# Softplus and SiLU as single ScalarE activations, and new durations and lags for the kernel's list scheduler

## The chip, the cores and the metric

The kernel runs on one core of one Trainium2 chip. The metric is the device time of one execution in microseconds, the median of several. The core has TensorE (PE, matrix multiplication into PSUM), VectorE (DVE), ScalarE (ACT), GpSimd (POOL) and SyncE (SP), whose queue issues all the DMAs of this kernel.

## The reference

```python
# q, k, v: [2, 8, 768, 64]; proj: [64, 6]
mask = bucket(q @ proj) == bucket(k @ proj)       # 6 sign bits for each row
scores = where(mask, q @ k.T / sqrt(64), -1e9)
attn = exp(scores - max) / (sum + 1e-9)
x = (attn @ v) as [1536, 512]                      # heads side by side
h = x @ w_in                                       # [512, 2048]
g = maximum(h, 0) + log1p(exp(-abs(h)))            # softplus
x = g @ w_out                                      # [2048, 512]
gate = x @ w_gate;  val = x @ w_val                # [512, 1536] each
out = (gate * 1 / (1 + exp(-gate)) * val) @ w_out2 # [1536, 512]
```

The weights come as 64-bit floats, read as pairs of 32-bit words.

## The kernel before

The 1536 rows are cut into four chunks of 384 (two batches, two halves each). Three stages follow each other, with overlap:

- Attention: for each batch, head and 128-row tile ("unit", 96 in all) PE makes the scores into PSUM tile `z`, DVE takes their minimum or maximum (`mx`, L888/L893), ACT takes the exponential with its row sum (`ex`, L909), the result is turned (on PE, or split in two f16 halves by ACT/POOL and turned by a DMA, `PT<-P`), and PE applies the values (`pv`). Chunk 0 works in fp32, the others with f16 halves.
- First feed-forward (`ffn1`, once for each chunk): 16 tiles of 128 hidden rows x 384 columns, twelve f16 matmuls each (L1134 to L1136, in the helper `three`), into a PSUM bank of ring `f` or, in batch 1, of `f` and `z` by turns (two banks each). The softplus of a tile is: Abs on ACT (`mag`, L1161), relu on DVE or ACT (`relu`, L1166), Exp and Ln on ACT (`ex`, L1177; `ln`, L1180), their sum on DVE (`add`, L1183), then a high half (`hi`, L1188 on ACT, L1194 on POOL) and a low half (`lo`, L1197 on POOL) in f16. Then four accumulations of 48 matmuls each with `w_out`.
- Gated unit: the products with `w_gate` and `w_val` are Strassen products of 2 x 2 blocks, for which batch p's input is first scaled, subtracted and split (`parts7`, L1274 to L1323), and each weight piece too (`split7`). `pair_of` runs for each batch and each of six column groups: seven products per matrix, their sums by ACT (`keep`, L1463) and DVE (`plus`, L1468), then for four tiles a Sigmoid (L1497/L1499), a multiplication with the gate itself, one with the value (`mul`, L1502; `mul_raw`, L1505, for the tile that is still in PSUM), the halves (L1510, L1513), and the last products with `w_out2` (L1537 to L1539) that DVE adds up (L1553).

The weights of the first feed-forward come in 16 pieces: two DMAs into the one buffer `raw64a`, three integer operations on DVE (L408, L413, L419) that make 32-bit floats, a sum of squares on ACT and a one-column matmul on PE for the scale (`total`, L359), and the two halves (L446 to L462).

The order of all instructions is made by a list scheduler when the program is built (`Order`). A step has an urgency, one or several ways to run (engine, cost in us, function, and perhaps a bonus or malus from the table `BV`), the steps it comes after, and the buffers it takes from rings of fixed size. `run` keeps a model of when each engine is free, takes the steps that could start first, and among those that start within SLACK of the first the one with the lowest urgency; each engine gets its instructions in that order and then runs them in order on the chip. `LAT` is the lag from an engine's end to another's start ("EA": PE to ACT; W and V are both DVE), `dve`, `stt`, `act`, `gps`, `gts` and `pe` are costs of an operation of n columns, `U` shifts the urgency of kinds of steps, and `T0`, `GAP`, `LEAD`, `W1_GAP`, `W2_GAP` set when units and weight pieces come due.

Of the kernel before, what the change touches and what calls it, by code (L numbers as in the profile page):

```python
# [55 lines left out]
class Order:  # L56
# [132 lines left out]
def tile_hash_attention__softplus_ffn__silu_glu(  # L189
# [54 lines left out]
    BV = dict(ck=0.865, re=1.809, st=-2.309, tf=0.612, th=1.227, hi=2.138, lo=5.114, slo=0.082, wlo=0.046, bits=-0.999, meas=1.623, cv=-0.593, ca=0.592)  # L244
    U = dict(st=0, vl=0, tp=-20.24, th=-2, tl=-1.85, w2=51.64, qp=-7.63, kp=-4.93, kv=3.56, f1=0.25, y=40, ev=-5.28, ex=2.63, hi=-7.89, lo=2.67, gw=422.36, x=3.11)
# [1498 lines left out]
```

## Time and profile before

| | us |
|---|---|
| median of 3 runs (lowest, highest) | 880.66 (879.75, 881.27) |
| the profiled execution | 882.55 |
| its span, first to last instruction | 880.6 |
| mean granted clock of TensorE | 0.972 of full speed |

The rows below are of that one execution. PE's busy time counts matmuls in flight; they overlap, so the duration of one is longer than the time from one to the next. A granted clock below 1.00 in a stretch is the share of full speed that was granted over that stretch; the levels are 1.0 (2.4 GHz) and 0.5 (1.2 GHz).

### The profile page before, as it was taken

What the parts mean: (1) busy time and instruction counts of PE and PEld (TensorE: products, weight loads), DVE (VectorE), ACT (ScalarE), POOL (GpSimd) and SP (SyncE); (2) the same over time, 40 slices, a digit from 0 to 9 for tenths busy, and PEclk for the clock granted to TensorE, in tenths of its full rate; (3) what the DMA queues carried; (4) which work ended last, traced back from release to release, by engine and by line L of the source; (5) the groups of instructions that cost most, each with busy time, mean ns of one, the idle gap of its engine ahead of it and who ended that gap; (6) DMA issues with size and microseconds to landing.
All of it is one profiled execution on the core that took longest, in us unless ns stands there. A gap on an engine that the chain in (4) does not pass through costs nothing.

```text
span 880.6 us, 14652 instructions
## 1 busy us (share of the span) xinstructions
PE 811.8 (92%) x5436; PEld 517.1 (59%) x5436; DVE 653.8 (74%) x1188; ACT 501.9 (57%) x966; POOL 473.1 (54%) x453
## 2 busy tenths in 40 slices
PE   7999899889989988998889998995899999999998
PEld 4666567456555655565556565563566566666666
DVE  4788687979896769879547798329858989694445
ACT  3455365568887677885667658335455545353331
POOL 0001111769786678885668737416745675764332
PEclk9999799989999999999989999998999999999999
DMA  6244344856778887666773421000312121200003
GB/s 203 75 132 136 114 115 118 170 124 128 169 131 169 163 163 136 103 88 128 129 130 58 156 96 49 1 1 8 136 48 95 49 96 48 96 1 1 1 1 143
DMA packets 179191, 86.05 MB, mean 98 GB/s; under 512 B 141104, under 2 KB 165808, under 8 KB 179120
## 3 DMA queue, kind: packets, MB, share of 16 engines
q1 hardware_dynamic: 179120, 85.12, 41.2%
q8 instruction: 42, 0.69, 0.3%
q14 instruction: 29, 0.24, 0.1%
HBM read 47.35 MB, written 3.15 MB: 57 GB/s over the span
## 4 chain that ended last, share of the span: by engine, by line
PE 46%; DVE 27%; DMA 12%; POOL 5%; issue 5%; ACT 3%; SPq 1%; DVEq 0%; POOLq 0%; ACTq 0%
DMA PT<-P 7%; PE z L1134 5%; PE z L1136 5%; PE z L1135 5%; PE z L869 4%; PE f L1537 3%; PE f L1539 3%; PE f L1538 3%; PE f L602 3%; DVE fr L1183 2%; PE pv L966 2%; DMA raw64a<-in_moe_w_in_dram 2%; POOL P L929 2%; DVE E L888 2%; DVE fr L1166 2%
## 5 line engine op out<-in xcount | busy, mean ns | idle before, releaser
L929 POOL TENSOR_TENSOR P<-E,P 128x768 f16<-128x768 f32 x72 | 123.6, 1718 | 14.0 <-ACT P L916 10.5
L1502 POOL TENSOR_TENSOR sg<-cc,sg 128x384 f32<-128x384 f32 x45 | 51.0, 1144 | 69.8 <-DVE cc L1468 32.9
L869 PE MATMUL z<-k,q 128*128 128x384 f32 x192 | 81.4, 554 | 3.5 <-DVE E L888 3.5
L1134 PE MATMUL z<-y,w 128*128 128x384 f16 x216 | 71.4, 331 | 12.3 <-DVE cc L1468 4.2
L1197 POOL TENSOR_TENSOR g<-fr,g 128x384 f16<-128x384 f32 x64 | 67.1, 1055 | 17.3 <-ACT g L1188 13.2
L1463 ACT ACTIVATE cc<-z,smalls 128x384 f32<-128x384 f32 x72 | 40.4, 576 | 55.2 <-PE z L1136 54.9
L1513 POOL TENSOR_TENSOR sT<-sg,sT 128x384 fp32r<-128x384 f32 x48 | 59.8, 1263 | 21.4 <-ACT sT L1510 21.4
L1136 PE MATMUL z<-y,w 128*128 128x384 f16 x216 | 71.2, 330 | 0.0
L1135 PE MATMUL z<-y,w 128*128 128x384 f16 x216 | 71.2, 330 | 0.0
L1134 PE MATMUL f<-xy,w1h 128*128 128x384 f16 x192 | 63.9, 333 | 2.5 <-DVE smalls L371 1.4
L1537 PE MATMUL f<-wo,sT 128*128 128x512 f32 x144 | 62.2, 432 | 3.3 <-DVE acc L1553 2.6
L909 ACT ACTIVATE E<-E,st 128x768 f32<-128x768 f32 x48 | 44.7, 931 | 35.3 <-DVE E L888 33.3
L1135 PE MATMUL f<-xy,w1h 128*128 128x384 f16 x192 | 64.0, 333 | 0.0
L1136 PE MATMUL f<-xy,w1l 128*128 128x384 f16 x192 | 63.9, 333 | 0.0
L966 PEld LDWEIGHTS <-PT 128*128 128x128 f16 x1296 | 47.4, 100 | 25.2 <-DMA PT<-P 15.2
L1183 DVE SCALAR_TENSOR_TENSOR fr<-fa,smalls,fr 128x384 f32<-128x384 f32 x64 | 56.0, 886 | 6.3 <-ACT fa L1180 4.0
L966 PE MATMUL pv<-v,PT 128*128 128x64 f16 x1296 | 51.4, 196 | 10.0 <-DMA PT<-P 9.6
L1539 PE MATMUL f<-wo,sT 128*128 128x512 f32 x144 | 56.4, 392 | 0.0
L1538 PE MATMUL f<-wo,sT 128*128 128x512 f32 x144 | 56.3, 391 | 0.0
L888 DVE TENSOR_SCALAR_CACHE_REDUCE E<-z 128x768 f32<-128x768 f32 x48 | 45.5, 953 | 14.5 <-PE z L869 9.0
L1135 PEld LDWEIGHTS <-w 128*128 128x128 f16 x336 | 33.2, 99 | 36.7 <-issue 18.8
L1553 DVE TENSOR_TENSOR acc<-f,acc 128x512 f32<-128x512 f32 x60 | 41.2, 687 | 16.6 <-PE f L1539 14.9
(253 smaller groups left out, 2288.7 us busy)
## 6 DMA issues: line engine op xcount, KB each, us to landing
raw64a<-in_moe_w_in_dram SPq DMA_DIRECT2D x16, 512.0 KB, 4.4
raw64a<-in_moe_w_out_dram SPq DMA_DIRECT2D x16, 512.0 KB, 5.0
raw64b<-in_moe_w_gate_dram SPq DMA_DIRECT2D x12, 512.0 KB, 4.4
raw64b<-in_moe_w_val_dram SPq DMA_DIRECT2D x12, 512.0 KB, 4.7
raw64b<-in_moe_w_out_dram SPq DMA_DIRECT2D x12, 512.0 KB, 4.4
rawk<-in_k_dram SPq DMA_DIRECT2D x19, 192.0 KB, 2.8
rawv<-in_v_dram SPq DMA_DIRECT2D x19, 192.0 KB, 2.9
rawq<-in_q_dram SPq DMA_DIRECT2D x16, 192.0 KB, 3.9
```

The source lines that it names most:

```text
L869: nc.tensor.matmul(a[:, x, 0:HS], lhsT=plain(qd["q"])[:, ts], rhs=plain(kd["k"])[:, x * HS:(x + 1) * HS], start=True, stop=True,)
L888: nc.vector.tensor_scalar(new(att, [128, 2, HS], F32, E), z.t[:, :, 0:HS], PLAIN_TOP, None, op0=ALU.min, op1=ALU.min, accum_out=a[:, 1:2],)
L929: return lambda: eng.tensor_tensor(P.t[:, 1, :], E.t.rearrange("p a b -> p (a b)"), P.t[:, 0, :], op=ALU.subtract)
L966: nc.tensor.matmul(pv.t[:, t, :], lhsT=PT.t[:, w, kk, :], rhs=values.t[:, kk, c0:c0 + D], start=(kk == 0 and w == 0 and c0 == 0), stop=(kk ...
L1134: nc.tensor.matmul(ps, lhsT=wh, rhs=xh, start=first, stop=False, skip_group_check=onto)
L1135: nc.tensor.matmul(ps, lhsT=wh, rhs=xl, start=False, stop=False, skip_group_check=onto)
L1136: nc.tensor.matmul(ps, lhsT=wl, rhs=xh, start=False, stop=last, skip_group_check=onto)
L1183: nc.vector.scalar_tensor_tensor(out=fr.t, in0=fa.t, scalar=sc[b]["sg"], in1=fr.t, op0=ALU.mult, op1=ALU.add)
L1197: return lambda: eng.tensor_tensor(g.t[:, 1], fr.t, g.t[:, 0], op=ALU.subtract)
L1537: nc.tensor.matmul(f.t, lhsT=sT.t[:, 0, cs], rhs=wh, start=(r == 0), stop=False)
L1538: nc.tensor.matmul(f.t, lhsT=sT.t[:, 0, cs], rhs=wl, start=False, stop=False)
L1539: nc.tensor.matmul(f.t, lhsT=sT.t[:, 1, cs], rhs=wh, start=False, stop=(r == 1))
```

## The change

In batch 1 the softplus is one Softplus activation into `fa`; the high half is taken from it with the scale `sg` (ACT, POOL or DVE), the low half by one scaled subtraction on DVE or two operations on POOL. Each Softplus comes after all Exp and Ln steps that were made before it (`all_exps`): those of attention, and of batch 0's softplus, which stays as it was. In the gated unit Sigmoid and the multiplication with the gate become one Silu. The scheduler's lags, its cost functions, many single costs, `BV`, `U` and the due times have new numbers. The core of the diff (single costs of other steps change in the same manner):

```diff
-    LAT = {"EE": 0.0, "AA": 0.15, "GG": 0.1, "VV": 0.13, "EA": 0.2, "EV": 0.2}
+    LAT = {
+        "EE": 0.0, "AA": 0.15, "GG": 0.1, "VV": 0.13, "EA": 0.22, "EV": 0.2, "EG": 0.25, "AV": 0.125, "VA": 0.115,
+        "GV": 0.035, "GA": 0.035, "AG": 0.17, "VG": 0.23, "AE": 0.145, "VE": 0.135, "GE": 0.06,
+    }
...
     def act(n):
-        return 0.28 + n / 1400.0
+        return 0.09 + n / 1200.0
     def gps(n):
-        return 0.1 + n / 510.0
+        return 0.143 + n / 526.0
     def gts(n):
-        return 0.05 + n / 1050.0
+        return 0.28 + n / 1211.0
...
-    BV = dict(ck=0.865, re=1.809, st=-2.309, tf=0.612, th=1.227, hi=2.138, lo=5.114, slo=0.082, wlo=0.046, bits=-0.999, meas=1.623, cv=-0.593, ca=0.592)
-    U = dict(st=0, vl=0, tp=-20.24, th=-2, tl=-1.85, w2=51.64, qp=-7.63, kp=-4.93, kv=3.56, f1=0.25, y=40, ev=-5.28, ex=2.63, hi=-7.89, lo=2.67, gw=422.36, x=3.11)
+    BV = dict(ck=0.788, re=0.248, st=-4.032, tf=1.16, th=-3.479, hi=3.915, lo=12.565, slo=-0.738, wlo=-0.612, bits=-4.056, meas=4.769, cv=-0.383, ca=0.101)
+    U = dict(st=-1.482, vl=-21.844, tp=-33.571, th=-50.907, tl=14.878, w2=44.101, qp=4.699, kp=-5.538, kv=0.27, f1=16.662, y=42.77, ev=-43.888, ex=6.594, hi=-11.632, lo=13.78, gw=250.452, x=2.144)
...
-            s = x = step(u + U["ex"], "A", act(S) + 0.39, ex, [s], uses=[E, st, sums], line="ex")
+            s = x = step(u + U["ex"], "A", act(S) + (0.2 if PLAIN[b] else 0.29), ex, [s], uses=[E, st, sums], line="ex")
+            all_exps.append(x)
...
-                s = step(u + U["tp"], "E", 6 * 0.14, turn, [s], takes=[T], uses=[E], line="tp")
+                s = step(u + U["tp"], "E", 0.68, turn, [s], takes=[T], uses=[E], line="tp")
...
+            def soft(gi=gi, f=f, fa=fa):
+                nc.scalar.activation(
+                    new(gpool, [128, CN], F32, fa), f.t[:, 0:CN], AF.Softplus, scale=sc[b]["inv"][:, gi:gi + 1]
+                )
+            def thi_a(fa=fa, g=g):
+                nc.scalar.activation(g.t[:, 0], fa.t, AF.Copy, scale=sc[b]["sg"])
...
+            def tlo_v(fa=fa, g=g):
+                nc.vector.scalar_tensor_tensor(
+                    out=g.t[:, 1], in0=fa.t, scalar=sc[b]["sg"], in1=g.t[:, 0], op0=ALU.mult, op1=ALU.subtract
+                )
+            def tlo_g(fa=fa, g=g):
+                nc.gpsimd.tensor_scalar(fa.t, fa.t, sc[b]["sg"], 1.0, op0=ALU.mult, op1=ALU.mult)
+                nc.gpsimd.tensor_tensor(g.t[:, 1], fa.t, g.t[:, 0], op=ALU.subtract)
...
+            if b == B - 1:
+                a = step(U["f1"], "A", act(CN) + 0.07, soft, [s, g_ready] + exps, takes=[fa], uses=[f])
+                a = ways(U["f1"], [("A", act(CN) + 0.09, thi_a), ("G", gts(CN), thi_g), ("W", dve(CN, 2), thi_v)], [a], uses=[fa, g])
+                g_done.append(ways(U["f1"], [("G", gts(CN) + gps(CN), tlo_g), ("W", stt(CN), tlo_v)], [a], uses=[fa, g]))
+                continue
...
-            a = step(U["f1"], "A", act(CN) + 0.04, ln, [a], uses=[fa])
+            a = step(U["f1"], "A", act(CN) + 0.1, ln, [a], uses=[fa])
+            all_exps.append(a)
...
-            return ways(u, [("W", dve(n) + 0.05, go(nc.vector)), ("G", gps(n) + 0.15, go(nc.gpsimd), BV["lo"])], after)
+            return ways(u, [("W", dve(n) + 0.05, go(nc.vector)), ("G", gps(n), go(nc.gpsimd))], after)
...
-                    nc.scalar.activation(t, tg.t, AF.Sigmoid)
+                    nc.scalar.activation(t, tg.t, AF.Silu)
...
-            for n, t, e in (("g", tg, None), ("v", tv, ends[1][j])):
-                if raw:
-                    s = step(0, "V", stt(CN) + 0.08, mul_raw(n, t), [s, e], uses=[t, sg])
-                else:
-                    s = ways(0, [("W", dve(CN), mul(nc.vector, t), 0.3), ("G", gps(CN) + 0.1, mul(nc.gpsimd, t))], [s, e], uses=[t, sg])
+            if raw:
+                s = step(0, "V", stt(CN), mul_raw, [s, ends[1][j]], uses=[tv, sg])
+            else:
+                s = ways(0, [("W", dve(CN), mul(nc.vector)), ("G", gps(CN), mul(nc.gpsimd))], [s, ends[1][j]], uses=[tv, sg])
...
-    T0, GAP, LEAD, W1_GAP, W2_GAP = 12, 2.65, 12.351, 5.974, 6.601
+    T0, GAP, LEAD, W1_GAP, W2_GAP = 15.591, 2.644, 12.522, 4.542, 2.827
```

## Rows read from the trace of the kernel before

**Rows 1.** The page's busy shares: us, share of the span, instructions.
```profile
PE 811.8 (92%) x5436; PEld 517.1 (59%) x5436; DVE 653.8 (74%) x1188; ACT 501.9 (57%) x966; POOL 473.1 (54%) x453
```

**Rows 2.** Stages: length, busy us of PE, PEld, DVE, ACT, POOL, clock, DMA share, GB/s.
```profile
22.00:154.00 132.00, 123.60 (x671) 86.94 (x672) 104.39 (x216) 68.22 (x122) 16.23 (x21) 0.95 0.37 115
154.00:449.00 295.00, 267.72 (x2399) 163.00 (x2397) 232.47 (x465) 210.93 (x434) 216.22 (x205) 0.97 0.75 140
449.00:586.00 137.00, 131.07 (x867) 79.09 (x866) 87.78 (x124) 83.95 (x167) 78.01 (x80) 0.98 0.26 67
...
594.00:616.00 22.00, 12.90 (x63) 6.52 (x61) 21.79 (x29) 12.38 (x21) 14.40 (x9) 0.84 0.03 4
...
638.00:858.00 220.00, 213.91 (x1167) 140.58 (x1167) 161.05 (x250) 99.75 (x177) 121.67 (x111) 0.99 0.13 44
```

**Rows 3.** The same view: two stretches of 22 us in the first feed-forward.
```profile
528.00:550.00 22.00, 19.27 (x109) 11.08 (x107) 18.41 (x28) 18.46 (x37) 17.31 (x19) 0.92 0.14 49
572.00:594.00 22.00, 22.00 (x138) 13.38 (x137) 4.37 (x11) 8.07 (x16) 3.03 (x2) 1.00 0.00 1
```

**Rows 4.** Groups of PE, 449 to 586: count, busy us, mean ns, idle before.
```profile
L966 PE MATMUL pv<-v,PT 128*128 128x64 f16 x92 | 3.7, 194 | 0.9 <-DMA PT<-P 0.9
```

**Rows 5.** Groups of ACT, 449 to 562, by form.
```profile
L1180 ACT ACTIVATE fa<-fa,smalls 128x384 f32<-128x384 f32 x32 | 19.4, 612 | 0.5
L1177 ACT ACTIVATE fa<-fa 128x384 f32<-128x384 f32 x32 | 16.4, 518 | 0.5
L1161 ACT ACTIVATE fa<-z,smalls 128x384 f32<-128x384 f32 x16 | 9.2, 577 | 5.3 <-DVE fr L1183 4.7
```

**Rows 6.** Groups of DVE, 449 to 562, by form.
```profile
L1183 DVE SCALAR_TENSOR_TENSOR fr<-fa,smalls,fr 128x384 f32<-128x384 f32 x32 | 24.7, 777 | 3.0 <-ACT fa L1180 0.9
L1166 DVE TENSOR_SCALAR fr<-z,smalls 128x384 f32<-128x384 f32 x16 | 9.8, 613 | 8.3 <-POOL g L1197 6.7 <-ACT fa L1161 1.5
```

**Rows 7.** Groups of POOL over the span.
```profile
L1197 POOL TENSOR_TENSOR g<-fr,g 128x384 f16<-128x384 f32 x64 | 67.1, 1055 | 17.3 <-ACT g L1188 13.2 <-PE pv L966 1.0 <-DVE xp L582 0.6
...
L1502 POOL TENSOR_TENSOR sg<-cc,sg 128x384 f32<-128x384 f32 x45 | 51.0, 1144 | 69.8 <-DVE cc L1468 32.9 <-DVE sg L1502 19.9 <-ACT sg L1499 16.8
...
L1194 POOL TENSOR_SCALAR g<-fr 128x384 f16<-128x384 f32 x34 | 19.8, 586 | 15.2 <-DVE fr L1183 15.1
```

**Rows 8.** Groups of DVE over the span: the two multiplications.
```profile
L1502 DVE TENSOR_TENSOR sg<-cc,sg 128x384 f32<-128x384 f32 x27 | 17.6, 662 | 3.0 <-ACT sg L1499 3.0
...
L1505 DVE SCALAR_TENSOR_TENSOR sg<-z,smalls,sg 128x384 f32<-128x384 f32 x24 | 14.6, 610 | 0.5 <-PE z L1136 0.5
```

**Rows 9.** ACT in order of time: start us, us, then the instruction.
```profile
451.57 0.58 ACT L1161 ACTIVATE fa<-f,smalls 128x384 f32<-128x384 f32 x1 [0.18 <-PE f L1136]
...
453.66 0.19 ACT L909 ACTIVATION_READ_ACCUMULATOR E<-E,st,smalls 128x1 f32 x1
```

**Rows 10.** PE in order of time, with its idle time.
```profile
543.30 0.38 PE L359 MATMUL f<-smalls 128*128 128x1 f32 x2 [1.28 <-DVE fr L1166]
545.13 0.32 PE L1134 MATMUL f<-xy,w1h 128*128 128x384 f16 x1 [1.44 <-DVE smalls L371]
```

**Rows 11.** Groups of PE, 594 to 616.
```profile
L1134 PE MATMUL z<-y,w 128*128 128x384 f16 x19 | 6.9, 365 | 9.1 <-DVE sg L1505 4.1 <-ACT cc L1463 3.4 <-DVE cc L1468 1.6
```

**Rows 12.** ACT in order of time, around the table load.
```profile
597.99 1.28 ACT L1499 ACT_TABLE_LOAD   x1
599.28 0.52 ACT L1499 ACTIVATE sg<-cc 128x384 f32<-128x384 f32 x1
```

**Rows 13.** One line, L408: ns min/median/max, first and last start.
```profile
L408 DVE TENSOR_SCALAR w32a<-raw64a x16: 679/694/1584, 10.2 to 223.1; 128x1024 int32<-128x1024 int32 x16
```

**Rows 14.** Groups of DVE, 22 to 154: the other operations of a weight piece.
```profile
L419 DVE SCALAR_TENSOR_TENSOR w32a<-raw64a,w32a 128x1024 int32<-128x1024 int32 x11 | 13.8, 1251 | 0.2
L413 DVE SCALAR_TENSOR_TENSOR w32a<-raw64a,w32a 128x1024 int32<-128x1024 int32 x11 | 13.5, 1223 | 0.1
L462 DVE SCALAR_TENSOR_TENSOR w1l<-w32a,smalls,w1h 128x1024 f16<-128x1024 f32 x8 | 10.2, 1278 | 0.7 <-POOL w1h L458 0.7
```

More of the change, by code (lines that the diff above doesn't have):

```diff
@@ L359, in go @@
             nc.tensor.matmul(f.t[:, 0:n], lhsT=ones_mat, rhs=t, start=True, stop=True)
-        return order.step(urgency, [("E", 0.45, go)], after, [f]), f
+        return order.step(urgency, [("E", 0.22, go)], after, [f]), f
     def pow2(r):
@@ L642, in planes @@
         for x, f in enumerate(ps):
-            s = step(u, "E", pe(4 * HS if plain else 2 * HS), products(x, f), after, takes=[f], uses=uses)
-            b = ways(u, [("V", dve(HS) + 0.14, bits(x, f), BV["bits"]), ("A", act(HS), signs(x, f))], [s],
+            s = step(u, "E", 0.85 if plain else 0.4, products(x, f), after, takes=[f], uses=uses)
+            b = ways(u, [("V", dve(HS) + 0.14, bits(x, f), BV["bits"]), ("A", act(HS) + 0.09, signs(x, f))], [s],
                      takes=[hb[x]], uses=[f] + uses)
@@ L781, in copy @@
             return go
-        s = step(u, "E", 6 * 0.14, turn, [ld[0]], takes=[T, kk], uses=[raw[0]], line="tk")
-        s = ways(u, [("A", act(S) - 0.05, copy(nc.scalar.copy)), ("V", dve(S) + 0.07, copy(nc.vector.tensor_copy), BV["ck"])],
+        s = step(u, "E", 0.68, turn, [ld[0]], takes=[T, kk], uses=[raw[0]], line="tk")
+        s = ways(u, [("A", act(S) - 0.04, copy(nc.scalar.copy)), ("V", dve(S) + 0.07, copy(nc.vector.tensor_copy), BV["ck"])],
                  [s], uses=[T, kk])
@@ L807, in copy_v @@
             nc.vector.tensor_scalar_mul(plain(qq)[0:64], T.t[0:64, 0:CN], -1.0 / float(D) ** 0.5)
-        s = step(u, "E", 3 * 0.14, turn, [ld], takes=[T, qq], uses=[raw], line="tq")
-        s = ways(u, [("A", act(CN), copy_a), ("V", dve(CN) + 0.13, copy_v, BV["ck"])], [s], uses=[T, qq])
+        s = step(u, "E", 0.36, turn, [ld], takes=[T, qq], uses=[raw], line="tq")
+        s = ways(u, [("A", act(CN) + 0.02, copy_a), ("V", dve(CN) + 0.05, copy_v, BV["ck"])], [s], uses=[T, qq])
         pl = planes(u + U["qp"], 1, 1, lambda: plain(qq)[0:64], lambda: plain(qq), [s, proj_ready], [], [qq], True)
@@ L849, in tile_hash_attention__softplus_ffn__silu_glu @@
     xn_open = {}
+    all_exps = []
     turned = []
@@ L985, in apply_f @@
                     )
-            s = step(u, "E", pe((8 if PLAIN[b] else 4) * HS), qk, kd["ready"] + qd["ready"], takes=[z], uses=[kd["k"], qd["q"]],
+            s = step(u, "E", 1.32 if PLAIN[b] else 0.68, qk, kd["ready"] + qd["ready"], takes=[z], uses=[kd["k"], qd["q"]],
                      line="qk", behind=turned[-2:-1])
-            s = step(u, "V", dve(S) + 0.15, mx, [s, first, hs.get("iv")],
+            s = step(u, "V", dve(S) + 0.1, mx, [s, first, hs.get("iv")],
                      takes=[st, E] + ([sums] if t == 0 else []), uses=[z] + ([sums] if t else []), line="mx")
@@ L1492, in pair_of, with silu, mul, mul_raw @@
             raw = j == 2
[L1494 removed]
+            def silu(tg=tg, sg=sg, raw=raw):
                 t = new(late["f2"], [128, CN], F32, sg)
                 if raw:
[L1497 removed]
+                    nc.scalar.activation(t, tg.t[:, 0, 0:CN], AF.Silu, scale=gvs[b, "g"][:, mp:mp + 1])
                 else:
[L1499 to L1506 removed]
+                    nc.scalar.activation(t, tg.t, AF.Silu)
+            def mul(eng, sg=sg, tv=tv):
+                return lambda: eng.tensor_tensor(sg.t, tv.t, sg.t, op=ALU.mult)
+            def mul_raw(sg=sg, tv=tv):
+                nc.vector.scalar_tensor_tensor(
+                    out=sg.t, in0=tv.t[:, 0, 0:CN], scalar=gvs[b, "v"][:, mp:mp + 1], in1=sg.t, op0=ALU.mult, op1=ALU.mult
                 )
@@ L1692, in finish @@
             s = step(due, "A", act(n), hi_a, [s, f2_open], takes=[slot], uses=[w32], line="wo")
-            return None, ways(due, [("G", gps(n) + 0.1, lo(nc.gpsimd)), ("W", dve(n), lo(nc.vector), BV["lo"])], [s], uses=[w32, slot])
+            return None, ways(due, [("G", gps(n), lo(nc.gpsimd)), ("W", dve(n), lo(nc.vector), BV["lo"])], [s], uses=[w32, slot])
         return finish
```

87 lines of the change are left out of this document (42 added, 45 removed).

## The prediction

> **What bounds the kernel now.** I read the page's busy shares first: TensorE (PE) has a matmul in flight for 92% of the span, VectorE (DVE) works 74%, ScalarE (ACT) 57%, GpSimd (POOL) 54% [rows 1]. An average over stages says little, so next I cut the span into stages [rows 2]. The reader is to see three things there. From 22 to 449 us (attention of both batches, with the first feed-forward of batch 0 fitted in) PE is without a matmul for 132.00 - 123.60 + 295.00 - 267.72 = 35.7 us, and the granted clock is 0.95 and 0.97: the missing 5% and 3% are 6.6 + 8.9 = 15.5 us of clock, which is the time lost if all of it was spent at the lower level (1.2 GHz) with PE full. From 449 to 586 (first feed-forward of batch 1) DVE, ACT and POOL are all under 65% busy, so PE is the bound. In 594 to 616 PE has 12.90 us and DVE 21.79 of 22: there DVE is the bound. From 638 to 858 PE is idle 6.1 us of 220: the gated unit there runs at PE's pace.
>
> Busy PE is not PE at its peak, so I take the peak from a stretch that is full: 138 matmuls, nearly all of 384 columns, in 22 us at clock 1.00 are 0.159 us each [rows 3]. In 449 to 586 there are 867 matmuls, 92 of them short attention ones [rows 2, 4]; the other 775, all but a few of 384 columns, need 123 us. The 92 short ones, at their share of a pipelined run, add about 3 us (estimate; their 194 ns of [rows 4] overlap). So 137 - 126 = 11 us of that stage is lost. In 594 to 616 the 63 matmuls need 10.0 us, so 12.0 is lost.
>
> **Part A, Softplus for batch 1.** Removed for each of 32 tiles: on ACT Abs (577 ns), Exp (518) and Ln (612); on DVE the relu (613) and the sum (777) [rows 5, 6]. Added: one Softplus on ACT. The trace has no Softplus; every 384-wide activation in the group takes 518 to 612 ns whatever its function, and the one with the same operands (PSUM in, a scale from a tile) takes 577, which I use. So ACT sheds 32 x (0.518 + 0.612) = 36.2 us. DVE sheds 32 x (0.613 + 0.777) = 44.5 us, and takes back at most 32 x 0.78 = 25 us if all low halves go to it. The low half goes to POOL today at 1055 ns [rows 7]; there it now needs the scaling too, 586 + 1055 = 1.64 us, so the planner will give most to DVE, and POOL sheds up to 34 us. None of that is time by itself: a tile needs 12 x 0.159 = 1.91 us of PE, and ACT spends 1.71 us on it now. What it buys is the waits of PE that these operations end: ahead of 543.30 PE stands 1.28 us for a DVE relu and ahead of 545.13 it stands 1.44 us for small DVE operations behind the next relu [rows 10], and that window's clock is 0.92, or 1.8 us of 22 [rows 3]. I take the two gaps and the clock, and half a microsecond for smaller waits on the relu: -5. Bounds: 0 (if weight pieces keep DVE busy at the same places) and -11 (everything lost).
>
> **Part A's new wait.** A Softplus waits for every Exp and Ln planned so far, that of the last attention unit too. Queued behind it on ACT in program order is whatever the planner put there; who waits is PE, for the PSUM banks that unread tiles hold: two "f" and two "z". In the run the first Abs of chunk 2 starts at 451.57 and the last Exp's accumulator read ends at 453.85 [rows 9]. With a table load behind that (1.28 us [rows 12]) the first Softplus starts at 455.1, 3.6 us later than today's Abs. Four banks are four tiles, 7.6 us of PE, so in today's order the banks cover it and the cost is 0. They no longer do so if chunk 2's tiles are ready more than 7.6 us ahead of the last Exp, and a held "z" bank is one that the last attention units, which also use two, don't have. I take +1; bounds 0 and +8 (three more units of the run of Exps, at the planner's 2.64 us of spacing).
>
> Of the load, the row says that the old gated stage's one load took 1.28 us, from 597.99 to 599.27, and the Sigmoid ran right behind it [rows 12]. The Trainium skill ("ScalarE: Activation LUTs", What ACT_TABLE_LOAD costs) puts a switch at about 2.66 us, since it counts a drain of 1.38 us beside the load. By the row the added switch costs ACT 1.3 us, by the page 2.7; with the four-bank cover the sum is the same to within 1.4 us, and the trace shows no such drain.
>
> **Part B, Silu.** Sigmoid and Silu are one activation each, with one table load; what goes is the first of two multiplications for each of 48 tiles. 12 are the DVE form at 610 ns (half of the 24): 7.3 us. 36 are half of the 72 L1502, 45 on POOL at 1144 ns and 27 on DVE at 662: (51.0 + 17.6) / 72 = 0.95 us each, 34.3 us [rows 7, 8]. In 594 to 616 PE's 9.1 us of waits end on exactly these: 4.1 on the raw multiplication, 3.4 on the ACT copy, 1.6 on the DVE add [rows 11]. The raw tile's bank is freed by the Silu instead of the multiplication behind the sigmoid, about one DVE operation sooner (0.6 to 0.9 us), and DVE has some 3 us less to do. But most of DVE's 21.79 us is the preparation of batch 1's Strassen operands, which stays. I take -3; bounds -12 (all lost there) and +4 (the new plan puts three or four POOL operations of 1.14 us ahead of what PE waits for). In 638 to 858 only 6.1 us can be had; I take -2, bounds -6 and 0, since POOL and DVE are off PE's path there.
>
> **Part C, the planner's numbers.** Outside A and B no operation is added or removed; what changes is order and which engine takes an operation with several ways. The old costs were off: a 384-wide activation was planned at 0.28 + 384/1400 = 0.55 us and takes 0.52 and, back to back, less; the POOL scaling was planned at 0.42 + 0.06 and takes 0.586 [rows 5, 7]. With ACT cheaper and its bonus "re" cut from 1.81 to 0.25, more relus of batch 0 go to ACT: each takes 0.61 us off DVE. Where it can pay is 22 to 449, where 35.7 us of gaps and 15.5 us of clock lie. The errors were tens of nanoseconds against steps of 0.5 to 2 us, and DVE is 79% busy there in each part [rows 2], so I expect few of the gaps to go: -6. Bounds: -51 (all) and +19, the slow rival below.
> The same part moves transfers: the pieces of w_in and w_out come due every 4.5 and 2.8 us instead of 6.0 and 6.6, and w_out starts at 44 instead of 52. Each piece has two DMAs on SP's queue, and they are moved past the loads of k, q and v; the one raw64a buffer holds each next pair until DVE has read the last, which limits how far they can run ahead. I cost the DMAs at nothing, covered by the DMA share of 0.37 in 22 to 154 [rows 2]; without the cover a late q, k or v would stop a unit.
>
> **Sum.** -5 + 1 - 3 - 2 - 6 = -15. The profiled execution took 882.55 us (span 880.6 and 1.95 around it): 867.5. The median of the runs is 880.66, 1.89 less: **866**. Adding the ends of all terms gives far more than the chance of them meeting, so the range is made from the cases below.
>
> **Rivals.**
> 1. The plan gains a lot. If half of the 51 us of gaps and clock in 22 to 449 goes, C is -25, the sum -34: 847. For it: no engine is full there, so the losses are order. Against: DVE's 79% is in bursts, and PE can't wait less than its DVE reader.
> 2. The gate eats the gain. The last Exp comes late against chunk 2, four banks are full, and the tail of attention runs with one "z" bank: +8 instead of +1, and nothing from C: -5 + 8 - 3 - 2 = -2: 879. For it: an f1 tile of batch 1 is already there ahead of the last Exp; against: 3.6 us stand against 7.6 us of cover.
> 3. Slower: weight pieces crowd early attention. A piece costs DVE 0.69 + 1.22 + 1.25 + 1.28 = 4.4 us [rows 13, 14]. 16 pieces run from 10.2 to 223.1 us; 11 lie in 22 to 154, one ahead, so four lie behind 154. Brought ahead of 154 they are 4 x 4.4 = 18 us more for a DVE that is busy 104 of 132 us, in the one stretch where PE has no feed-forward to fill with; nothing comes back if the later stretch is held by POOL (216 of 295 us) as much as by DVE. +18 and -9 from the others: 890. It decides when more than about half of that work lands where DVE has no idle time; for it: the new gaps of 2.8 us; against: the single raw64a buffer.
> 4. It doesn't do what it says: Softplus needs its own table, and the Squares between its tiles switch it back and forth. Row: the old gated stage has Sigmoid, Square and Copy in turn and one load [rows 12]. The trace has no Softplus to tell the same of its set; six alternations of two loads would be 12 x 1.28 = 15 us of ACT, inside the 36 it sheds, with some stalls of PE: 870. The Trainium skill ("ScalarE: Activation LUTs", Table sets: the hidden batching unit) says that cheap functions stand in every set; by that rule there is one more load and nothing else, and the Sigmoid row agrees.
>
> **How the numbers follow.** Forecast (856 to 874, with rival 4 in it): 0.44. Rival 1 (under 856): 0.20. Rival 2 (874 to 882): 0.15, of which 0.07 is within 0.2%, that is within 1.8 us of 880.66, about what a measurement of this kernel can tell from no change. Rival 3 (over 882): 0.21. So faster 0.44 + 0.20 + 0.08 = 0.72, same 0.07, slower 0.21. The range goes from 846, just under rival 1, to 887, short of rival 3's price: about 0.08 is left out below and 0.11 above. The forecast's own range is 856 to 874.
>
> **What would show it.** A: in the profile after, between the first Softplus and the gated unit, PE without the two gaps and with a clock near 1.00; 32 fewer Exps and Lns. Gate: PE's idle time just ahead of the first Softplus, and who ends it. B: PE's idle in the 20 us behind the last feed-forward matmul, now 9.1 us. C: the time of the last Exp, now 453.85; if it is over 460 rival 3 is right, under 435 rival 1. I am wrong altogether if the stages behind the last Exp get longer, or if more than three table loads show.

## The result and the profile after

The changed kernel takes 847.58 us (median of four runs, 843.72 to 850.67); the kernel before, on the same chip, 880.2. The ratio is 0.9631 [0.9586, 0.9676], or 32.6 us less. The direction is as forecast and the time lies inside the range (846 to 887), but below the forecast's own 856 to 874, and the change is more than twice the 15 us of the sum: as a forecast of size it was wrong.

I cut every profile into four stages at the same events: 22 us; chunk 0's first feed-forward matmul; chunk 2's first one (in these two profiles the last Exp of attention is beside it; in others it comes up to 18 us earlier); the end of the last `w_out` matmul of chunk 3; the end. For the profiled executions (882.55 and 850.67 us):

| us | early attention | late attention | feed-forward of batch 1 | gated unit | span |
|---|---|---|---|---|---|
| before | 147.1 | 280.0 | 137.3 | 294.2 | 880.6 |
| after | 134.1 | 277.5 | 129.2 | 286.2 | 849.0 |
| difference | -13.0 | -2.5 | -8.1 | -8.0 | -31.6 |

The page's busy shares of after, to set against [rows 1]: POOL sheds 128 us and DVE 41.5, ACT almost nothing.

```profile
PE 794.6 (94%) x5436; PEld 511.7 (60%) x5436; DVE 612.3 (72%) x1151; ACT 499.9 (59%) x950; POOL 344.8 (41%) x320
```

The view by stretches (length, then busy us of PE, PEld, DVE, ACT, POOL, the granted clock, DMA share, GB/s), first of the kernel before, for its two attention stages as cut here:

```profile
22.00:169.10 147.10, 136.33 (x737) 93.49 (x737) 118.44 (x234) 76.21 (x136) 28.07 (x30) 0.94 0.41 118
169.10:449.10 280.00, 255.09 (x2333) 156.52 (x2333) 218.51 (x447) 202.94 (x420) 204.47 (x196) 0.97 0.75 140
```

Then of after; the last three lines answer to the last three of [rows 2]:

```profile
22.00:156.10 134.10, 129.09 (x759) 91.27 (x760) 116.26 (x237) 86.02 (x153) 19.12 (x23) 0.97 0.49 133
156.10:433.60 277.50, 250.35 (x2328) 155.29 (x2328) 214.81 (x434) 224.01 (x458) 176.42 (x160) 0.98 0.75 142
433.00:563.00 130.00, 128.73 (x868) 78.72 (x869) 70.44 (x116) 53.24 (x100) 22.36 (x21) 1.00 0.24 67
571.00:593.00 22.00, 16.99 (x88) 9.47 (x88) 21.37 (x38) 13.03 (x24) 8.17 (x7) 0.92 0.14 48
...
615.00:827.00 212.00, 209.39 (x1150) 138.24 (x1149) 145.66 (x234) 96.58 (x172) 95.90 (x85) 1.00 0.13 43
```

In early attention PE's idle time went from 10.8 to 5.0 us and the clock's share (the part of full speed that was not granted, times the length) from 8.8 to 4.0: 10.6 of the 13.0 us. In batch 1's feed-forward PE is idle 1.3 us of 130 at full clock, where it was idle 5.9 of 137 at 0.98. The gated unit starts at 0.92, where it was 0.84, and then has a full clock.

**Softplus.** Groups of PE of after from 433 to 563 us (busy us, mean ns, then idle before and what ended it): the matmuls of the tiles and of `w_out` wait for nothing (the one wait that the stage has, 1.1 us, is ahead of a scale matmul of a weight piece).

```profile
L1139 PE MATMUL z<-g,w2h 128*128 128x384 f16 x128 | 41.7, 326 | 0.0
...
L1139 PE MATMUL f<-xy,w1h 128*128 128x384 f16 x64 | 20.9, 326 | 0.1
```

Groups of ACT of after, 433 to 545, by form. A Softplus takes 578 ns, as taken from the Abs of [rows 5]; seven high halves are ACT's, the other 25 DVE's.

```profile
L1182 ACT ACTIVATE fa<-f,smalls 128x384 f32<-128x384 f32 x16 | 9.3, 579 | 13.7 <-PE f L1141 13.0 <-DVE g L1196 0.7
L1182 ACT ACTIVATE fa<-z,smalls 128x384 f32<-128x384 f32 x16 | 9.2, 578 | 15.1 <-PE z L1141 15.1
L1335 ACT ACTIVATE junk<-xy 128x384 bf16<-128x384 f32 x12 | 6.2, 518 | 0.2
L1187 ACT ACTIVATE g<-fa,smalls 128x384 f16<-128x384 f32 x7 | 4.3, 615 | 0.2
```

Groups of DVE of the same stretch: all 32 low halves went to DVE, none to POOL.

```profile
L1196 DVE SCALAR_TENSOR_TENSOR g<-fa,smalls,g 128x384 f16<-128x384 f32 x32 | 21.4, 670 | 5.2 <-ACT g L1187 4.4
L1190 DVE TENSOR_SCALAR g<-fa,smalls 128x384 f16<-128x384 f32 x25 | 10.4, 418 | 17.2 <-ACT fa L1182 17.2
```

ACT of after in order of time (start, duration, instruction): the gate that the forecast priced. The last Exp's accumulator is read at 433.32, the table loaded at 435.74, and the first Softplus runs at 437.04. PE's groups above show that nobody waited.

```profile
433.32 0.19 ACT L913 ACTIVATION_READ_ACCUMULATOR E<-E,st,smalls 128x1 f32 x1
...
434.89 0.83 ACT L920 CAST P<-E 128x768 f16<-128x768 f32 x1 [1.39 <-DMA PT<-P]
435.74 1.28 ACT L1182 ACT_TABLE_LOAD   x1
437.04 0.58 ACT L1182 ACTIVATE fa<-f,smalls 128x384 f32<-128x384 f32 x1
437.65 0.61 ACT L1187 ACTIVATE g<-fa,smalls 128x384 f16<-128x384 f32 x1
```

The whole trace has three table loads, at 0.79, 435.74 and 579.68 us; the twelve Squares (L1335) between Softplus tiles cause none, so rival 4 is out. The Trainium skill ("ScalarE: Activation LUTs", Table sets: the hidden batching unit) has cheap functions in every set; the trace agrees for Copy (the seven of L1187) and for Square, which that section of the Trainium skill doesn't list.

**Silu.** Of 96 multiplications 48 are left; POOL's of after over the span, to set against [rows 7]:

```profile
L1536 POOL TENSOR_TENSOR sg<-cc,sg 128x384 f32<-128x384 f32 x14 | 17.0, 1226 | 42.0 <-ACT sg L1533 31.2 <-PE f L1572 8.0 <-DVE cc L1502 2.8
```

and DVE's, against [rows 8]:

```profile
L1536 DVE TENSOR_TENSOR sg<-cc,sg 128x384 f32<-128x384 f32 x22 | 15.2, 690 | 0.7
...
L1539 DVE SCALAR_TENSOR_TENSOR sg<-z,smalls,sg 128x384 f32<-128x384 f32 x12 | 7.3, 608 | 0.0
```

Where PE stood 9.1 us at the start of the gated unit, 4.1 of them for the raw multiplication [rows 11], it now stands 6.2, and no multiplication is among what ended it there (PE of after, 571 to 593):

```profile
L1139 PE MATMUL z<-y,w 128*128 128x384 f16 x24 | 8.3, 348 | 6.2 <-ACT cc L1497 4.9 <-ACT sg L1531 0.9 <-DVE cc L1502 0.5
```

### The profile page after: what moved, and what is told of

Its sections match the earlier page's. It is cut to its first block, busy times and chain, and to the rows that moved or that the text cites. A ratio compares the mean times of both kernels' runs of the same rounds, so it can differ in the third digit from the quotient of the medians.

```text
span 849.0 us, 14355 instructions
## 1 busy us (share of the span) xinstructions
PE 794.6 (94%) x5436; PEld 511.7 (60%) x5436; DVE 612.3 (72%) x1151; ACT 499.9 (59%) x950; POOL 344.8 (41%) x320
## 4 chain that ended last, share of the span: by engine, by line
PE 35%; DVE 11%; ACT 5%; DMA 3%; POOL 3%; issue 2%; SPq 0%; POOLq 0%; DVEq 0%; ACTq 0%
PE z L1139 6%; PE z L1141 6%; PE z L1140 6%; PE f L1570 3%; PE f L1572 3%; PE f L1571 3%; DMA PT<-P 2%; DVE w L1420 2%; DVE cc L1502 1%; PE f L1139 1%; PE f L1140 1%; PE f L1141 1%; PE y L1139 1%; PE y L1141 1%; PE y L1140 1%
## 5 line engine op out<-in xcount | busy, mean ns | idle before, releaser
L873 PE MATMUL z<-k,q 128*128 128x384 f32 x192 | 76.8, 528 | 3.1 <-DVE E L892 3.0
L1139 PE MATMUL z<-y,w 128*128 128x384 f16 x216 | 71.2, 329 | 8.5 <-ACT cc L1497 6.4
L1139 PE MATMUL f<-xy,w1h 128*128 128x384 f16 x192 | 63.9, 333 | 7.0 <-DVE fr L1171 4.1
L897 DVE TENSOR_SCALAR_CACHE_REDUCE E<-z 128x768 f32<-128x768 f32 x48 | 45.5, 948 | 18.7 <-POOL P L933 18.4
L920 ACT CAST P<-E 128x768 f16<-128x768 f32 x57 | 47.0, 825 | 20.1 <-DMA PT<-P 20.0
L892 DVE TENSOR_SCALAR_CACHE_REDUCE E<-z 128x768 f32<-128x768 f32 x48 | 45.6, 952 | 11.5 <-PE z L873 7.5
L1502 DVE SCALAR_TENSOR_TENSOR cc<-z,smalls,cc 128x384 f32<-128x384 f32 x48 | 29.2, 613 | 34.1 <-PE z L1141 17.9
```

The costliest lines, as they stand in the source:

```text
L873: nc.tensor.matmul(a[:, x, 0:HS], lhsT=plain(qd["q"])[:, ts], rhs=plain(kd["k"])[:, x * HS:(x + 1) * HS], start=True, stop=True,)
L892: nc.vector.tensor_scalar(new(att, [128, 2, HS], F32, E), z.t[:, :, 0:HS], PLAIN_TOP, None, op0=ALU.min, op1=ALU.min, accum_out=a[:, 1:2],)
L920: nc.scalar.copy(P.t[:, 0, :], E.t.rearrange("p a b -> p (a b)"))
L1139: nc.tensor.matmul(ps, lhsT=wh, rhs=xh, start=first, stop=False, skip_group_check=onto)
```

## The experiments

All kernels by the four stages of their profiled execution (us), with the median and the ratio to the kernel before on the same chip. The chips differ, so ratios are compared and not medians. A stage is read from one execution, and that scatters: ahead of chunk 2, before and e1 to e3 share one order of instructions and after, e6, e13 and e14 another, and their early attention differs by up to 5 us.

| kernel | early | late | feed-forward | gated | median us | ratio, 95% |
|---|---|---|---|---|---|---|
| before | 147.1 | 280.0 | 137.3 | 294.2 | 880.2 | |
| after | 134.1 | 277.5 | 129.2 | 286.2 | 847.58 | 0.963 [0.959, 0.968] |
| e1_softplus | 142.3 | 278.9 | 129.9 | 290.9 | 869.88 | 0.991 [0.987, 0.995] |
| e2_silu | 142.2 | 276.3 | 137.6 | 287.2 | 873.65 | 0.996 [0.992, 1.000] |
| e3_both | 142.6 | 277.9 | 130.1 | 287.4 | 862.39 | 0.986 [0.978, 0.995] |
| e4_new_costs_old_knobs | 136.5 | 291.2 | 126.4 | 286.5 | 865.58 | 0.987 [0.981, 0.993] |
| e5_old_costs_new_knobs | 161.0 | 266.7 | 128.1 | 286.9 | 866.86 | 0.989 [0.984, 0.994] |
| e6_numbers_only | 134.9 | 272.8 | 134.7 | 292.7 | 856.58 | 0.977 [0.972, 0.983] |
| e7_before_slack | 147.3 | 274.6 | 135.9 | 292.3 | 873.01 | 0.996 [0.993, 1.000] |
| e8_after_slack | 135.7 | 283.7 | 130.4 | 287.8 | 861.04 | 0.983 [0.978, 0.987] |
| e9_after_slack_down | 132.3 | 283.5 | 132.2 | 285.7 | 856.92 | 0.979 [0.973, 0.985] |
| e10_after_port | 136.0 | 289.8 | 129.0 | 286.0 | 864.09 | 0.985 [0.981, 0.989] |
| e11_both_slack_down | 146.6 | 291.3 | 127.1 | 286.0 | 874.81 | 0.998 [0.995, 1.001] |
| e12_both_port | 145.2 | 288.4 | 127.9 | 288.0 | 876.56 | 0.998 [0.995, 1.002] |
| e13_act_chain_back | 134.2 | 272.8 | 131.9 | 286.4 | 850.6 | 0.969 [0.964, 0.975] |
| e14_dve_work_back | 130.2 | 272.7 | 133.8 | 285.8 | 847.99 | 0.969 [0.963, 0.975] |
| e15_search_a | 131.8 | 277.4 | 136.0 | 299.6 | 867.47 | 0.989 [0.985, 0.994] |
| e16_search_b | 136.1 | 271.1 | 141.5 | 296.7 | 868.98 | 0.989 [0.985, 0.993] |
| e17_act_pool_costs | 165.7 | 276.9 | 130.4 | 285.7 | 878.89 | 1.001 [0.997, 1.006] |
| e18_pe_costs_lags | 130.2 | 288.1 | 132.1 | 287.9 | 863.05 | 0.982 [0.976, 0.988] |

**The operations and the numbers apart.** Theory: most of the gain is the planner's numbers. Rival: the operations. e1 puts the Softplus branch into the kernel before, at old costs; e2 the Silu; e3 both; e6 is the changed kernel with the old operations.

```diff
+            if b == B - 1:                                     # e1, e3: into before
+                a = step(U["f1"], "A", act(CN), soft, [s, g_ready] + exps, takes=[fa], uses=[f])
...
-                    nc.scalar.activation(t, tg.t, AF.Sigmoid)  # e2, e3: into before
+                    nc.scalar.activation(t, tg.t, AF.Silu)
...
-            if b == B - 1:                                     # e6: out of after
-                a = step(U["f1"], "A", act(CN) + 0.07, soft, [s, g_ready] + exps, takes=[fa], uses=[f])
...
-                    nc.scalar.activation(t, tg.t, AF.Silu)
+                    nc.scalar.activation(t, tg.t, AF.Sigmoid)
```

> Softplus in batch 1 alone, with its gate; all old costs, lags, malus and due times. Theory 1 (the gain of a stage comes from what is edited in it): from the first feed-forward matmul of chunk 2 to the last of chunk 3 it takes 129 us instead of 137, as in the changed kernel; nothing else moves by more than 3 us; time 872. Rival (any edit re-deals the whole order, and the gains are such deals): the last Exp or the gated unit moves by more than 5 us either way, though nothing is edited there. Second rival (the gate costs): PE stands more than 2 us ahead of the first Softplus.

> Silu alone; all old numbers. Theory 1: from the last feed-forward matmul to the end of the span 286 us instead of 294, everything ahead of it as before; time 872. Rival 1 (the forecast's size): 289 us, time 875. Rival 2 (the planner's numbers, not the Silu, shortened the gated unit): 293 us or more, time 879.

> Softplus and Silu, all old numbers. Theory 1: the two stages' gains add up to 16 us and the last Exp stays near 454: time 864. Rival (the numbers make it all): 875 or more. Rival (re-dealt order): attention moves by more than 5 us.

> All new numbers with the old operations (four activations for the softplus, Sigmoid and two multiplications). Theory 1 (attention's gain is the numbers'): last Exp near 434, the two later stages as before (137 and 294), time 864. Rival (operations and numbers gain in the same places): last Exp later than 445, or the later stages within 3 us of the changed kernel's 129 and 286.

The stages came out as the theory had them: e1's feed-forward at 129.9 us (129 expected), e2's gated unit at 287.2 (286; by the forecast's size 289), e6's two later stages at 134.7 and 292.7 (137 and 294). The marks of a re-dealt order came in by number too, since chunk 2 starts 5.9 to 8.6 us earlier in e1 to e3 than in before; but the order up to there is the same instruction for instruction (last section).

The four corners fit together: the operations are worth 1.4% at the old numbers (e3, 0.986) and 1.5% at the new ones (0.963/0.977), 12 to 13 us; the numbers 2.3% either way, 20 us. So the theory holds, with the operations not small. Each operation acts in its own stage, one line from each of three kernels. e1 from chunk 2's first matmul on, PE full at 1.00:

```profile
443.20:573.10 129.90, 128.70 (x867) 78.58 (x868) 65.07 (x93) 58.08 (x108) 38.10 (x43) 1.00 0.28 71
```

e2, with the old chain, and then its gated unit:

```profile
440.50:578.10 137.60, 131.70 (x870) 79.43 (x869) 87.56 (x124) 83.99 (x168) 77.99 (x80) 0.98 0.26 67
578.10:865.30 287.20, 270.16 (x1460) 178.58 (x1458) 200.55 (x306) 126.64 (x226) 140.84 (x119) 0.99 0.16 56
```

e6, with the new numbers and the old chain:

```profile
429.70:564.40 134.70, 130.27 (x857) 78.71 (x854) 86.37 (x116) 90.02 (x186) 69.00 (x60) 0.99 0.22 64
```

Over the table, feed-forward takes 129.4 us in the mean of twelve kernels with Softplus (e13 to e16 left out, where work is put back or the plan is another; the twelve run from 126.4 to 132.2) and 136.4 in the four without: -7.0. The gated unit takes 286.7 in fourteen with Silu (without e15 and e16) and 292.5 in the four without: -5.8.

**Why Softplus helps.** Theory: the DVE relu that read the bank is gone. Rival: the chain on ACT is short. Neither run brings the old chain back whole: e13 puts two Copies of `fa` behind each Softplus, so that ACT has three in a row again; e14 puts back a DVE relu on the bank, and an operation on DVE that waits for it.

```diff
+                for _ in range(2):                                     # e13
+                    a = step(U["f1"], "A", act(CN) + 0.01, lambda fa=fa: nc.scalar.activation(fa.t, fa.t, AF.Copy), [a], uses=[fa])
...
+                r = step(U["f1"], "V", stt(CN), relu, [a, g_ready], takes=[fr], uses=[f])     # e14
+                a = step(U["f1"], "W", stt(CN) + 0.07, lambda fa=fa: nc.vector.scalar_tensor_tensor(
+                    out=fa.t, in0=fa.t, scalar=1.0, in1=fa.t, op0=ALU.mult, op1=ALU.max), [a, r], uses=[fa, fr])
```

> The changed kernel with two more 384-wide copies in place on ACT behind each Softplus of batch 1 (the ACT work and the length of the old chain come back, DVE and the bank stay relieved). From the first feed-forward matmul of chunk 2 to the last of chunk 3 the old kernel took 137 us, the changed one 129. Theory D (DVE's work and its hold on the bank made PE wait, as the forecast has it): still 129 to 131. Rival A (the shorter chain on ACT is what counts): 133 or more.

> The changed kernel with the old relu (a second reader of the PSUM bank) and one more in-place operation on DVE for each Softplus tile of batch 1. Theory D: the same stretch takes 134 us or more again, with PE's waits ended by DVE's relu. Rival A: 129 to 131.

The stage is 4.6 us longer in e14 (133.8, where 134 was the theory's mark) and 2.7 in e13 (131.9, between the two marks); with the whole old chain at the same numbers, in e6, it is 5.5 longer. In e14 the two waits of [rows 10] are back, one for the relu and one for small DVE operations behind it (PE in order of time):

```profile
507.45 0.38 PE L362 MATMUL f<-smalls 128*128 128x1 f32 x2 [0.90 <-DVE fr L1171]
508.51 0.32 PE L1139 MATMUL f<-xy,w1h 128*128 128x384 f16 x1 [0.68 <-DVE smalls L374]
```

So is the wait of a bank that the relu has not read yet (PE's groups of e14, 430 to 575; 0.0 in after):

```profile
L1139 PE MATMUL z<-g,w2h 128*128 128x384 f16 x128 | 41.7, 326 | 1.9 <-DVE fr L1171 1.9
```

In e13 PE has a single wait in the stage, 2.39 us. It ends on ACT's read of a full `w_out` bank, but ACT was not busy with the Copies: it stood 3.71 us for DVE, at a cast that its order put ahead of that read (PE, then ACT, in order of time).

```profile
478.83 0.32 PE L1139 MATMUL z<-g,w2h 128*128 128x384 f16 x1 [2.39 <-ACT xy L1267]
...
477.47 0.83 ACT L1317 CAST y<-xy 128x768 f16<-128x768 f32 x1 [3.71 <-DVE xy L1310]
478.21 0.57 ACT L1267 ACTIVATE xy<-z,smalls 128x384 f32<-128x384 f32 x1
```

So the theory is borne out: of 3.5 us of waits in e14, 2.8 end on the relu, while in e13 none ends on the three ACT operations in a row. Its 2.7 us come of where the planner put that cast, and its 131.9 lies among the 126.4 to 132.2 of the other Softplus kernels. In e6 the longest wait, 2.60 us, ends on ACT's square of a weight piece, which began 0.5 us behind DVE's last operation on that piece: there too DVE sets most of it.

**How much of the numbers is luck of the draw.** A small change of a constant gives another order by the same rules. Theory: the numbers describe the chip better, and nudged kernels stay fast. Rival: they are a fitted draw, and a nudge loses it. "Both" is e3.

```diff
-    SLACK = 0.1067
+    SLACK = 0.1167    # e7 on before, e8 on after; 0.0967: e9 on after, e11 on both
...
-    PORT = 0.75
+    PORT = 0.76       # e10 on after, e12 on both
```

> The kernel before with one planner constant nudged: SLACK 0.1167 instead of 0.1067. No operation, cost or due time changes; the order of ties does. It measures how far the order alone scatters. Theory 1 (the plan's quality is set by costs and knobs, scatter is small): within 4 us of 880. Rival (re-dealt order is worth as much as the change): more than 8 us either way.

> The changed kernel with SLACK 0.1167 instead of 0.1067. Theory 1: within 4 us of 848. Rival (the new numbers are fitted to one order, so a nudge loses part of the gain): 856 or more, with most of the loss ahead of the last Exp.

> The changed kernel with SLACK 0.0967 instead of 0.1067. Theory 2 (part of the gain ahead of the feed-forward of batch 1 is one well-fitted order; about 8 us of it are lost with any nudge): chunk 2 starts at 440, time 856 to 862. Rival (costs and knobs carry the gain, and the first nudge was an unlucky one): chunk 2 starts at 434, time 848.

> The changed kernel with PORT 0.76 instead of 0.75 (how much of a wait the planner sees for DVE and POOL on their shared port). Theory 2: chunk 2 starts at 438 or later, time 856 or more. Rival: 434 and 848.

> Softplus and Silu with all old numbers, SLACK 0.0967. Theory 2, its other half: orders from the old costs scatter too, and their mean is later than that of the new ones: chunk 2 starts between 440 and 455, time 860 to 874. Rival (old and new numbers give orders of one distribution, the changed kernel is only its best draw): starts and times fall among those of the two nudged changed kernels.

> Softplus and Silu with all old numbers, PORT 0.76. As for SLACK 0.0967: theory 2 a start of chunk 2 between 440 and 455 and 860 to 874, on average later than the nudged changed kernels; rival: among them.

Both are true, in different stages. By the ratios each nudge costs the changed kernel 1.6 to 2.2%, 14 to 19 us, with intervals that stand apart; that this is no matter of the chip, e13 and e14 bear out, which have after's order up to chunk 2 and ran on the chip of e8 (850.6 and 848.0 us, e8 861.0).

e3 loses 1.1 and 1.2%, 10 us, at the edge of its wider interval, a little more than was expected (874.8 and 876.6 us for 860 to 874); before's own nudge is no loss (0.996). Nudged against nudged, three orders and two, (mean 0.982 and 0.998) the new numbers still give 1.6%, 14 us.

But in the table early attention doesn't overlap: seven kernels with all the old numbers (before, e1 to e3, e7, e11, e12) have 142.2 to 147.3, mean 144.8; seven with all the new ones (after, e6, e8 to e10, e13, e14) 130.2 to 136.0, mean 133.9. That is -10.9, and since each seven hold only four different orders: -11.3 if each order counts once. Late attention is 274.6 to 291.3, mean 281.1, with the old and 272.7 to 289.8, mean 279.0, with the new (-2.1, or -0.4 if each order counts once): the nudges act there.

In e10 late attention is 12.3 us longer than in after, and PE idle 34.5 us of it for 27.2. Its PE groups show the wait that grew, for turned halves `PT` that come by DMA:

```profile
L970 PE MATMUL pv<-v,PT 128*128 128x64 f16 x1242 | 48.6, 195 | 15.0 <-DMA PT<-P 14.9
```

In after the same group, from 156 to 433.6 us:

```profile
L970 PE MATMUL pv<-v,PT 128*128 128x64 f16 x1170 | 45.6, 195 | 8.1 <-DMA PT<-P 7.9 <-DVE xn L1038 0.3
```

**Which numbers.** e4 is the changed kernel with `BV`, `U` and the due times of before; e5 is e3 with those of after. e17 is e4 without the new lags and the new costs of PE's steps, so that of the costs only ACT's, POOL's and DVE's are new; e18 is e3 with just those lags and PE's costs.

```diff
+    LAT = {"EE": 0.0, "AA": 0.15, ..., "AE": 0.145, "VE": 0.135, "GE": 0.06}   # e18: as in after
...
-        return order.step(urgency, [("E", 0.45, go)], after, [f]), f
+        return order.step(urgency, [("E", 0.22, go)], after, [f]), f
...
-            s = step(u, "E", pe(4 * HS if plain else 2 * HS), products(x, f), after, takes=[f], uses=uses)
+            s = step(u, "E", 0.85 if plain else 0.4, products(x, f), after, takes=[f], uses=uses)
...
-                s = step(u + U["tp"], "E", 6 * 0.14, turn, [s], takes=[T], uses=[E], line="tp")
+                s = step(u + U["tp"], "E", 0.68, turn, [s], takes=[T], uses=[E], line="tp")
...
-            s = pvs = step(u, "E", 1.6 if full else pe(18 * 64), apply_f if full else apply,
+            s = pvs = step(u, "E", 1.37 if full else 0.55, apply_f if full else apply,
```

> The changed kernel with its new costs and lags, but with the old malus table BV, the old urgencies U and the old due times. Theory 1a (true costs and lags give the better order): the last Exp is at 434 as in the changed kernel, time 848 to 852. Rival 1b (the malus, urgencies and due times do it): the last Exp is at 450 or later and the time is 862 or more.

> Softplus and Silu with the old costs and lags, but the new malus table, urgencies and due times. Theory 1a (true costs and lags give the order): near the kernel with both operations and old numbers, last Exp 450 or later, 864 or more. Rival 1b (the malus, urgencies and due times do it by themselves): last Exp near 434, 850. Rival 1c (the two sets fit only each other): slower than with all old numbers, the last Exp later than 454.

> Softplus and Silu with new costs for ACT, POOL and DVE only; lags, PE's costs, malus, urgencies and due times old. Ahead of the first feed-forward matmul of chunk 0, counted from 22 us, all runs with old costs took 142 to 147 us and all with new ones 130 to 137. Theory: the cheaper ACT does it (PT and key copies go to ACT, DVE's minimum comes sooner): 137 or less. Rival: PE's costs or the lags: 142 or more.

> Softplus and Silu with new PE costs and lags only; ACT, POOL, DVE costs, malus, urgencies and due times old. Theory (the cheaper ACT does it): 142 us or more from 22 us to chunk 0's first feed-forward matmul. Rival: 137 or less.

By the ratios neither half of the numbers beats e3 (0.987 and 0.989 for 0.986). But e3's own order is a good draw, each half is one draw, and so which half pays in time is not settled. e4's last Exp came at 432.0, as the theory of true costs had it, and its time as the rival had it: the last Exp tells little of the time. e5 came as that theory had it (866.9 for 864 or more).

By stage, my theory that a cheaper ACT in the plan shortens early attention fell: with the costs of ACT, POOL and DVE alone it is the longest of all. e17:

```profile
22.00:187.70 165.70, 148.70 (x766) 103.87 (x766) 123.04 (x246) 89.94 (x158) 29.13 (x27) 0.89 0.42 117
```

PE idles 17.0 us there and the clock takes 18.2. With PE's costs and the lags alone it idles 7.8 at full clock, e18:

```profile
22.00:152.20 130.20, 122.41 (x732) 87.94 (x731) 112.62 (x226) 77.79 (x137) 30.26 (x30) 1.00 0.47 134
```

The eleven kernels with new lags and PE costs have 130.2 to 136.5 us of early attention, the nine without 142.2 to 165.7. So it is the lags or PE's costs, and not the due times of the weight pieces, which are the old ones in e4 and e18. Which of the two it is was not separated. e18's ratio, 0.982, is also the mean of the three nudged kernels with all the new numbers; with one order of e18 that is a hint only.

**A better plan by its own measure.** I searched `BV`, `U`, the due times, SLACK and PORT for the earliest end by the planner's model; all of them differ from after, and the cut shows two. Theory: its end time says enough for the chip to follow. Rival: the gain is the model's only.

```diff
-    SLACK = 0.1067
-    PORT = 0.75
+    SLACK = 0.0999    # e15; e16: 0.0937
+    PORT = 0.249      # e15; e16: 0.342
```

> The changed kernel with malus, urgencies, due times, SLACK and PORT from a random search on the planner's own end time. If orders are draws and a better plan runs better: chunk 2 starts at 430 or earlier, time 838 to 846. Rival (what the planner gains by a smaller PORT is only its model's): no faster than 848, the gain lost in DVE and POOL operations that take longer beside each other.

> A second such search from another seed. Theory: 838 to 846. Rival: 848 or more.

The rival came true: 867.5 and 869.0 us where 838 to 846 were hoped for. Attention is as good as after's, but feed-forward and gated unit are 7 to 13 us longer each. e15's operation of a weight piece on DVE, 431 to 567 us, takes 1965 ns:

```profile
L1420 DVE SCALAR_TENSOR_TENSOR w<-w32b,smalls,w 128x1024 f16<-128x1024 f32 x3 | 5.9, 1965 | 0.0
```

It takes 1584 ns in after between 433 and 563:

```profile
L1420 DVE SCALAR_TENSOR_TENSOR w<-w32b,smalls,w 128x1024 f16<-128x1024 f32 x3 | 4.8, 1584 | 0.0
```

PORT is the planner's price for DVE and POOL working at once, and the search had lowered it. Three such operations make 1.1 us of the 6.8 that the stage lost. That the lower price is the cause of the rest is argued and not shown: no run changed PORT that far alone. No kernel beat the changed one.

## Why the prediction was right and where it was wrong

- **Part B, Silu: -5 forecast, -5.8 measured.** Right in size, and in both places: PE's idle time fell from 12.3 to 9.3 us in the first 52 us of the gated unit and from 9.8 to 6.5 behind. The raw multiplication ended 6.6 us of the waits ahead of L1134 in before, and 0.6 ahead of the same line (L1139) in after.
- **Part A, Softplus: -5 + 1 forecast, -7.0 measured.** Right in mechanism: the two gaps and the time at the lower clock went, as priced, and e14 brings both gaps back. The gate's +1 was 0: no wait of PE in 433 to 563 ends on it. The rest is size. The stage lost 8.6 us before (5.9 idle, 2.7 of clock) and 1.3 after, so that nearly all of the loss went and not 5 of it; the forecast's 11 us of loss was too high, since its 0.159 us for a matmul counts matmuls that stand only in part in their 22 us.
- **Part C, the numbers: -6 forecast.** This is the step that failed: "The errors were tens of nanoseconds against steps of 0.5 to 2 us, and DVE is 79% busy there in each part [rows 2], so I expect few of the gaps to go: -6." I had looked at ACT's and POOL's costs. With these (and DVE's) alone early attention got worse (e17), with PE's costs and the lags it got better (e18). PE's costs were off by up to 0.3 us: a pair of scale matmuls was planned at 0.45 and is now at 0.22, a turn 0.84 and 0.68, the fp32 value products 1.6 and 1.37. In the trace of before they take 0.16, 0.71 and 1.39 us (medians at full clock, from the first matmul of a step to the first of the next). Over the draws the numbers give -10.9 in early attention and -2.1 in late, -13.0 for -6; the gain of early attention is firm, that of late attention is within the draws.
- **The draw and the execution, not in the sum at all.** The stages' mean differences, -13.0 - 7.0 - 5.8 = -25.8, leave 5.8 of the 31.6 us between the two profiled spans. This is luck, of the order and of the execution: after's stages are 2.0 us under the means of its kind, before's 3.8 over (427.1 for 425.9 us of attention, 137.3 for 136.4, 294.2 for 292.5). Against its nudged neighbours alone the order of after is worth more, the 14 to 19 us above. Of the 17.6 us by which the forecast missed, Part C thus has 7.0, Part A and its gate 3.0, Part B 0.8, and most of the rest is this luck.
- **The rivals.** Rival 1 gave the right time (847) and its mark came in (last Exp at 433.5, under 435), but the mark is a poor one: the last Exp ends at 432.0 in e4 and 430.9 in e10, which take 865.6 and 864.1 us. That the time is right is in part luck. Its mechanism holds in direction: PE's idle time in attention fell from 35.7 to 32.2 us and the clock's share from 17.2 (by the stages as cut here) to 9.6, but that is 11 of 53 and not half. Rival 2: the gate cost nothing. Rival 3: the last piece of `w_in` came at 207 instead of 223 us [rows 13], twelve pieces between 22 and 154 us instead of eleven, and early attention still became shorter. Of "what would show it", every mark for A, B and C read as it should; I had given the large gain a chance of 0.20. The line of after for rival 3:

```profile
L411 DVE TENSOR_SCALAR w32a<-raw64a x16: 680/693/1404, 9.7 to 206.8; 128x1024 int32<-128x1024 int32 x16
```

## What to carry to other kernels

Where a list scheduler sets the order, read its plan for the engine that bounds the stage, and compare those costs and lags with the trace first: here PE's costs and the lags shortened the stage that PE's waits held up, and the costs of the engines behind it alone did not. Before a gain of a few per cent is credited to new planner numbers, nudge one constant on both sides: a single order is a draw, here worth 14 to 19 us. And be wary of a search whose objective contains one of its own knobs: here it gained nothing on the chip, though that this was the reason is not shown.

## What the runs showed of the hardware that was not expected

One instruction order does not give one time by stage. e1, e2 and e3 have before's order on every engine up to chunk 2, and chunk 2 starts at 449.1 in before and 443.2, 440.5 and 442.5 in them; e6, e13 and e14 have after's, and it starts at 433.6, 429.7, 429.0 and 424.9. Up to 8.7 us thus lie in the execution alone. Between before and e2 the clock accounts for it: up to chunk 2 before ran 33.4 us at the lower level and e2 15.9, and half of the difference is 8.7 us, where the starts are 8.6 apart. In before, the clock fell to its lower level (1.2 GHz) behind short waits of PE, about 1 us each, and stayed there for a stretch of 10.2 us. The view of 88 to 110 us of before:

```profile
88.00:110.00 22.00, 19.05 (x76) 12.34 (x76) 14.43 (x28) 7.82 (x15) 3.40 (x4) 0.77 0.37 114
```

and of e2, the same instructions in the same order, with 112 matmuls where before made 76:

```profile
88.00:110.00 22.00, 19.15 (x112) 13.88 (x110) 19.25 (x37) 12.54 (x22) 2.64 (x3) 1.00 0.42 127
```

The waits alone don't tell the two apart. PE stood for the same two things in both, for 1.06 and 0.95 us in before:

```profile
92.16 0.84 PE L774 MATMUL z<-ident,rawk 128*64 128x128 f32 x6 [1.06 <-DVE E L888]
...
97.59 2.23 PE L982 MATMUL pv<-rawv,PT 128*128 128x64 f32 x12 [0.95 <-ACT PT L974]
```

and for 1.07 and 0.79 us in e2, with the clock at 1.00 all through. What decides is open.

```profile
91.31 0.84 PE L774 MATMUL z<-ident,rawk 128*64 128x128 f32 x6 [1.07 <-DVE E L888]
...
96.59 1.55 PE L982 MATMUL pv<-rawv,PT 128*128 128x64 f32 x12 [0.79 <-ACT PT L974]
```
